# Chunks in pairs: one work item of 256 tokens in place of two of 128 in a gated linear attention with a maxout layer

**Chip, cores, metric.** One core of one Trainium2 chip. The time is device microseconds (us) of one execution, as the median of a kernel's runs. Runs marked slow are over 1.5% above the fastest run of the same kernel, or lie in a lower granted clock of TensorE; ratios use fast runs only. In what follows PE is TensorE, ACT is ScalarE, DVE is VectorE, POOL is GpSimd and SP is SyncE, which here only issues DMAs (SPq is its queue).

## The reference, cut

```python
# q, k, v, alpha: [B=4, H=8, S=768, D=48] float32
for t in range(S):
    state = alpha[:, :, t, :, None] * state + einsum('bhd,bhe->bhde', k[:, :, t], v[:, :, t])
    y[:, :, t] = einsum('bhd,bhde->bhe', q[:, :, t], state)
x = y.transpose(0, 2, 1, 3).reshape(3072, 384)
out = np.maximum(x @ w1, x @ w2) @ w_out          # w1, w2: [384, 1024], w_out: [1024, 384]
```

Both kernels use max(a, b) = b + relu(a - b): with m = w2 @ w_out, out = x @ m + relu(x @ (w1 - w2)) @ w_out. In the programs h is x @ (w1 - w2), g its relu, and op the sum that is stored. The recurrence is done in chunks of tokens: cumulative sums of log alpha by matmuls (cs), exps, q and k scaled by them (qt, kt), transposes (tp, copied to qk), masked scores (pt), a state carried from chunk to chunk (w, T), and y, which is evicted as xT.

## The kernel before, the parts that matter

An item is one chunk of 128 tokens, one token to a partition, all eight heads. There are 24 items.

```python
LD = 5                                         # loads are issued this many items ahead
def load(n):                                   # alpha, q, k, v of one chunk: rows of 192 bytes
    ...
        nc.sync.dma_start(out=t, in_=src[b, :, c*C:(c+1)*C, :].rearrange("h p d -> p h d"))

def a1(n):  nc.scalar.activation(out=logas[n % 2][:, :, 0:D], in_=loads[n][0], func=ACTF.Ln)
def p1(n):  # cs: one matmul of 384 columns, and four narrow ones (gcol)
def p4(n):  # y: v16 and T16 on 32-column tiles of the PE array, all 128 rows
...
def tstep(a, i, half):                         # op = x @ m + g @ w_out, in two halves
    ...
    if half:
        nc.scalar.copy(out=os_, in_=op)        # "outs"
        nc.sync.dma_start(out=out[t0 : t0 + C, :], in_=os_)
...
for n in range(1, NCG + 1):
    if n - 1 + LD < NCG:
        load(n - 1 + LD)                       # item n + 4, in turn n
    v1(n + 1)
    if n > 1:
        p4(n - 1); a3(n - 1)
    gap(1.05)                                  # about 1 us of h and op matmuls, from a list
    if n > 1:
        ready(n - 1)
    if n < NCG:
        a1(n + 2)                              # Ln of item n + 2
        p3(n); v3(n)
    vt(n + 1)
    gap(1.05)
    p2(n + 1); v2(n + 1)
    gap(1.05)
    p1(n + 2); a2(n + 2)
```

## Time and profile before

| | before |
|---|---|
| median of 3 runs | 163.26 us (163.16 to 163.41) |
| span of the profiled run, mean granted clock | 161.4 us, 0.989 |
| PE busy, matmuls | 139.1 us (86%), 2056 |
| one item of 128 tokens in the loop | 5.2 us, so 10.4 for two |
| load packets | 192 bytes, 15 ns each |

Three lines of the page complete them: the granted clock of PE by slices of a fortieth of the span, the chain of waits by engine, and the queue that brings instructions (packets, MB, share).

```profile
86.90 0.43 SPq L66 DMA_DIRECT2D af<-in_alpha_dram  x1
...
96.35 0.56 ACT L123 ACTIVATE loga<-af 128x384 f16<-128x384 f32 x1
```

### The profile page before, as it was taken

How to read it: one execution, taken by the hardware profiler on the slowest of the kernel's cores; microseconds unless marked ns; L12 is line 12 of the kernel's file. 1: busy time of each engine (PE TensorE's matmuls, PEld its weight loads, DVE VectorE, ACT ScalarE, POOL GpSimd, SP SyncE). 2: the span in 40 equal slices, each digit the busy share in tenths (PEclk: the TensorE clock that was granted, in tenths of full speed). 3: DMA queues.
4: the chain of work that ended last, by engine and by line, in shares of the span. 5: the costliest groups of instructions: out<-in, count | busy, mean ns of one | idle time of the engine just before them, and what ended most of it. 6: DMA issues, size and time to landing. Idle time of an engine off the chain costs nothing.

```text
span 161.4 us, 5077 instructions
## 1 busy us (share of the span) xinstructions
PE 139.1 (86%) x2056; PEld 95.2 (59%) x2056; DVE 92.9 (58%) x153; ACT 81.3 (50%) x216; POOL 91.5 (57%) x170
## 2 busy tenths in 40 slices
PE   0427169799996999999999999999999999999990
PEld 0316157467664667666766667666676667657660
DVE  4163962095668747866576766875587656841110
ACT  3302063564754574487338753775466557435341
POOL 7714555079867666777447767765376876700000
PEclk9999999999999599999999999999999999999999
DMA  5999999999989899989999979998989611012021
GB/s 106 278 411 389 275 201 162 195 188 173 199 158 235 176 201 160 225 175 231 204 224 180 222 154 236 196 230 177 216 168 220 129 55 49 0 53 97 17 84 51
DMA packets 104648, 28.65 MB, mean 178 GB/s; under 512 B 100272, under 2 KB 104368, under 8 KB 104368
## 3 DMA queue, kind: packets, MB, share of 16 engines
q1 hardware_dynamic: 104624, 28.32, 84.0%
q8 instruction: 16, 0.26, 0.7%
q14 instruction: 8, 0.07, 0.1%
HBM read 23.59 MB, written 4.72 MB: 175 GB/s over the span
## 4 chain that ended last, share of the span: by engine, by line
PE 78%; DMA 9%; ACT 3%; SPq 2%; issue 2%; DVE 2%; POOL 1%; ACTq 0%; DVEq 0%; POOLq 0%
PE h L308 22%; PE op L325 20%; DMA wof<-in_moe_w_out_dram 9%; PE op L322 8%; PE y L258 5%; PE pa L208 4%; PE y L252 3%; PE tp L192 3%; PE tp L190 3%; PE kv L217 3%; PE mp L296 2%; PE cs L130 2%; PE cs L134 2%; SPq L66 2%; DVE pt L231 1%
## 5 line engine op out<-in xcount | busy, mean ns | idle before, releaser
L157 DVE TENSOR_TENSOR qt<-qf,ep 128x384 f16<-128x384 f32 x24 | 24.4, 1016 | 34.4 <-ACT ep L146 34.4
L308 PE MATMUL h<-xT,wd 128*128 128x384 f16 (+2 forms) x264 | 40.2, 295 | 1.0 <-ACT g L313 0.6
L325 PE MATMUL op<-wo,g 128*128 128x384 f16 x192 | 38.5, 327 | 0.0
L158 POOL TENSOR_TENSOR kt<-kf,en 128x384 f16<-128x384 f32 x24 | 24.4, 1015 | 24.6 <-ACT en L145 21.1
L313 ACT ACTIVATE g<-h 128x384 f16<-128x384 f32 (+2 forms) x66 | 25.2, 410 | 10.7 <-PE h L308 10.4
L308 PEld LDWEIGHTS <-wd 128*128 128x128 f16 x264 | 22.0, 103 | 10.6 <-issue 2.6
L329 ACT COPY outs<-op 128x384 f32<-128x384 f32 x24 | 11.5, 479 | 30.9 <-PE op L325 30.9
L162 POOL CAST v<-vf 128x192 f16<-128x192 f32 x48 | 26.9, 587 | 0.0
L325 PEld LDWEIGHTS <-g 128*128 128x128 f16 x192 | 17.4, 98 | 11.1
L199 DVE COPY qk<-tp 128x1024 f16<-128x1024 f16 x24 | 16.6, 691 | 9.8 <-PE tp L192 9.0
L145 ACT ACTIVATE en<-cs 128x384 f32<-128x384 f32 x24 | 11.7, 489 | 15.7 <-PE cs L134 14.0
L176 POOL TENSOR_TENSOR T<-w,g 48x192 f16<-48x192 f32 x20 | 10.0, 501 | 14.4 <-DVE w L239 11.9
L231 DVE TENSOR_TENSOR pt<-pa,u 128x512 f16<-128x512 f32 x24 | 16.4, 685 | 2.9 <-PE pb L208 2.9
L130 PE MATMUL cs<-loga,cmat 128*128 128x384 f16 x24 | 8.1, 338 | 10.0 <-ACT loga L123 10.0
L231 DVE TENSOR_TENSOR pt<-pb,u 128x512 f16<-128x512 f32 x24 | 16.3, 678 | 0.0
L258 PE MATMUL y<-pt,v 128*32 128x128 f16 x576 | 15.7, 226 | 0.0
L322 PE MATMUL op<-m,xT 128*128 128x384 f16 x72 | 15.7, 327 | 0.0
L311 DVE TENSOR_SCALAR g<-h 128x384 f16<-128x384 f32 (+2 forms) x22 | 9.7, 440 | 10.3 <-PE h L308 10.3
L134 PEld LDWEIGHTS <-loga 128*112 128x112 f16 x96 | 9.1, 137 | 9.8 <-issue 7.8
L123 ACT ACTIVATE loga<-af 128x384 f16<-128x384 f32 x24 | 12.9, 539 | 1.8 <-DMA af<-in_alpha_dram 1.8
L265 ACT CAST xT<-y 128x384 f16<-128x384 f32 x24 | 11.8, 490 | 3.9 <-PE y L258 3.9
L258 PEld LDWEIGHTS <-v 128*32 128x32 f16 x576 | 11.8, 100 | 0.5 <-issue 0.4
(55 smaller groups left out, 185.5 us busy)
## 6 DMA issues: line engine op xcount, KB each, us to landing
af<-in_alpha_dram SPq DMA_DIRECT2D x24, 192.0 KB, 4.1
qf<-in_q_dram SPq DMA_DIRECT2D x24, 192.0 KB, 4.5
kf<-in_k_dram SPq DMA_DIRECT2D x24, 192.0 KB, 4.7
vf<-in_v_dram SPq DMA_DIRECT2D x24, 192.0 KB, 4.4
out_dram<-outs SPq DMA_DIRECT2D x24, 192.0 KB, 3.2
w2f<-in_moe_w_dram SPq DMA_DIRECT2D x1, 1536.0 KB, 8.1
w1f<-in_moe_w_dram SPq DMA_DIRECT2D x1, 1536.0 KB, 10.9
wof<-in_moe_w_out_dram SPq DMA_DIRECT2D x1, 1536.0 KB, 14.7
```

Source lines behind the costliest of these rows:

```text
L123: nc.scalar.activation(out=logas[n % 2][:, :, 0:D], in_=loads[n][0], func=ACTF.Ln)
L134: nc.tensor.matmul(cs[0:112, o : o + 2], lhsT=lp[:, r, 0:112], rhs=gcol, start=True, stop=True)
L157: nc.vector.tensor_mul(out=qts[n % 2][:, :, 0:D], in0=qf, in1=s["ep"])
L158: nc.gpsimd.tensor_mul(out=kts[n % 2][:, :, 0:D], in0=kf, in1=s["en"])
L162: nc.gpsimd.tensor_copy(out=v16[:, :, :, 32 * t : 32 * t + 16], in_=vp[:, t])
L199: nc.vector.tensor_copy(out=qk, in_=st[n]["tp"])
L231: nc.vector.tensor_mul(out=pt[:, t], in0=s["pp"][t], in1=ub)
L258: nc.tensor.matmul(y[32 * r : 32 * r + 32, i, :], lhsT=v16[:, r, i, 16 * t : 16 * t + 32], rhs=s["pt"][:, t, r, :], start=(first and t == ...
L308: nc.tensor.matmul(h[:, 0:W], lhsT=wd16[:, s, f * 128 : (f + 1) * 128], rhs=xT[:, s, a : a + W], start=(s == 0), stop=(s == 2))
L313: nc.scalar.activation(out=gts[a][:, f, 0:W], in_=h[:, 0:W], func=ACTF.Relu)
L322: nc.tensor.matmul(op, lhsT=xT[:, s, t0 : t0 + C], rhs=m16[:, s, :], start=(s == 0), stop=False)
L325: nc.tensor.matmul(op, lhsT=gts[a][:, f, i * C : (i + 1) * C], rhs=wo16[:, f, :], start=False, stop=(f == NF - 1))
```

## The change

Its intent: an item is two chunks, so that ACT, DVE and POOL run half as many instructions of twice the size, and load rows become 384 bytes by putting two neighbouring tokens on one partition. Scores, kv and y are cut into tiles of 64 rows of the PE array. The first two items are done by head halves, so that work starts before all of their data is there. The core of the diff, with cuts:

```diff
-    ldp = ctx.enter_context(tc.tile_pool(name="ldp", bufs=6))
+    ldp = ctx.enter_context(tc.tile_pool(name="ldp", bufs=4))
-    LD = 5
+    def load(n, parts=1):
+        ...                     # .rearrange("h (p j) d -> p h (j d)", j=2)
+    load(0, 2)                  # then the weights in halves, then
+    load(1, 2)
+    load(2)
+    load(3)
 ... p1: cs is eight matmuls of 192 columns (c11, c11, c11, c01 for each head half)
 ... p3: scores on 64x64 tiles, qk[64*t : 64*t+D, ...] and half the tokens (u) at a time
 ... p4: y from pt and v on 64x32 tiles, twice as many matmuls of the same streaming
+    prep_w2(0) ... p4(0); a3(0) ... fpair(0, 0..3) between the weights' casts
+    prep_wo()
+    a1(1, (0,)); p1(1, (0,)); prep_m(0); a1(1, (1,)); p1(1, (1,)); ...
+    for n in range(2, ND + 1):
+        load(n + 2)
+        v1(n + 1); v16(n + 1)
+        if n > 2: p4(n - 1); a3(n - 1)
+        tstep(n - (1 if n == 2 else 2), 1, 0)
+        a1(n + 2)
+        if n < ND: p3(n, 0); v3(n, 0)
+        tstep(n - (1 if n == 2 else 2), 1, 1)
+        if n < ND: p3(n, 1); v3(n, 1)
+        if n > 2: fpair(n - 1, 0); fpair(n - 1, 1)
+        ...                     # pkv(n), vw, vt, fpair 2 and 3, p2(n + 1), v2(n + 1)
+        if n > 2: tstep(n - 1, 0, 0)
+        p1(n + 2); a2(n + 2)
+        if n > 2: tstep(n - 1, 0, 1)
```

There are 12 items, and a turn of the loop stands for two turns of before.

## The prediction

> **What bounds the kernel now.** I read the page's busy line and slices, then a table by stage, then TensorE's timeline inside one period, then the timeline of the start.
>
> ```profile
> PE 139.1 (86%) x2056; PEld 95.2 (59%) x2056; DVE 92.9 (58%) x153; ACT 81.3 (50%) x216; POOL 91.5 (57%) x170
> ...
> PE   0427169799996999999999999999999999999990
> ...
> DMA  5999999999989899989999979998989611012021
> ```
>
> Rows of busy tenths: PE is low for 22 us, uneven to 57 us, then full. DMA is full too, up to 126 us, so a DMA bound has to be excluded. The table by stage (us; busy per engine) does it:
>
> ```profile
> 0.00:22.00 22.00, 7.31 (x82) 5.46 (x83) 11.71 (x20) 5.85 (x9) 11.75 (x25) 1.00 0.95 282
> ...
> 42.00:58.00 16.00, 14.31 (x250) 10.18 (x245) 11.33 (x21) 8.98 (x27) 11.47 (x22) 0.89 0.97 194
> ...
> 72.50:88.10 15.60, 15.60 (x249) 10.51 (x247) 10.53 (x16) 9.25 (x25) 9.16 (x17) 1.00 1.08 211
> ...
> 134.90:147.20 12.30, 12.30 (x203) 7.83 (x201) 6.23 (x10) 4.92 (x12) 4.75 (x9) 1.00 0.10 33
> ```
>
> From 57 us on, PE is covered completely while DVE, ACT and POOL are below 70%. The chain of waits runs through PE alone there. Three chunks take 15.6 us, **10.4 us for two chunks**. PE records overlap, so I took starts from the timeline:
>
> ```profile
> 73.80 0.33 PE L130 MATMUL cs<-loga,cmat 128*128 128x384 f16 x1
> 73.96 0.32 PE L134 MATMUL cs<-gcol,loga 128*112 128x2 f16 x4
> ...
> 74.84 1.15 PE L308 MATMUL h<-xT,wd 128*128 128x384 f16 x6
> 75.92 0.23 PE L208 MATMUL pa<-qk 48*128 48x128 f16 x1
> 75.93 0.23 PE L208 MATMUL pb<-qk 48*128 48x128 f16 x1
> ...
> 76.25 0.31 PE L217 MATMUL kv<-v,kt 128*64 128x48 f16 x8
> 76.49 0.66 PE L308 MATMUL h<-xT,wd 128*128 128x384 f16 x3
> ```
>
> A difference of starts is what a group costs: cs 0.16, gcol 0.25, y 0.63 (74.21 to 74.84), p3 0.43 with the gap ahead of it, kv 0.24, a 384-column matmul 0.163. Per two chunks: transposes 0.88, cs 0.33, gcol 0.5, y 1.26, p3 0.86, kv 0.40 (a sixth are skipped), h 2.62, op 22 x 0.163 = 3.58. Sum 10.43, which is the 10.4 seen: the loop holds work and no wait.
>
> The start loses most. All work of PE is 12 x 10.4 + 5 (weights) = 130 of 161.4 us; after 57 us about 4 are idle, so about 27 were lost before. The weights land last:
>
> ```profile
> 11.73 1.04 ACT L271 CAST w<-w2f 128x1024 f16<-128x1024 f32 x1 [5.60 <-DMA w2f<-in_moe_w_dram]
> ...
> 19.78 1.15 ACT L282 CAST wo<-wof 128x1152 f16<-128x1152 f32 x1 [3.85 <-DMA wof<-in_moe_w_out_dram]
> ...
> 21.41 0.48 PE L130 MATMUL cs<-loga,cmat 128*128 128x384 f16 x1 [4.62 <-ACT loga L123]
> ```
>
> [...]
> 1. [...]six h matmuls begun at 74.84 need 0.98, yet pa begins at 75.92, 0.10 later.
> 2. [...]pa and pb start 3 ns apart and a pair takes 56 ns; four 32-column tiles of y take 57 ns. No run yet has both axes at once with 32 columns.
> 3. [...]192-byte packets 15 ns, 1536-byte ones 65 ns, so by a straight line some 22 ns for 384 bytes (estimate), 280 GB/s against about 195 now.
> [...]
>
> **The change, part by part.**
>
> *Loads.* An item is 4096 packets x 22 ns / 16 = 5.7 us for two chunks, against about 8. In the loop that is off the path and worth nothing. At the start it means twice the data ahead of the weights: item 0 is moved by about 7.5 us, the weights at about 395 GB/s by 19.4 and landed by 20.6, near 1 us later than now.
>
> *PE in the loop, per item.* h, op and transposes stay. Scores: 32 matmuls of 64x64, four at once, 8 x 56 ns[...]: 0.86, as now. kv: 32, four at once, 0.45 (+0.05). y: 24 state matmuls 0.34, then 96 value matmuls on eight tiles, 12 x 57 ns = 0.68[...]: 1.25, as now. Twice the instructions for the same streaming. cs: eight matmuls of 192 columns, 8 x 0.082 = 0.66, **+0.33**, since each of two tokens of a partition needs both. gcol: eight, full 128 columns, 0.40 (-0.1). Sum **10.7 us** against 10.4: no saving on the engine that bounds.
>
> *Other engines, per item.* ACT saves in Ln, exp (four at 0.49 become two at 0.81) but takes all evictions of h (4 x 0.61); about 7.0 of 10.7. DVE: [...]copy 1.2, two masks of 1.2, w 0.7: 6.2. POOL about 7.5. All have slack, so fewer, larger instructions buy nothing by themselves.
>
> *A new wait.* PSUM units are two, of two banks. cs(n+2) needs one that v2(n+1) or the last w has just emptied. v2 is now one copy of 2048, [...]1.2 us (1024 took 0.69), starting 0.2 after the transposes. PE has one half-step of op, 0.98, between. So PE waits 1.45 - 0.98, **about 0.5 per item**; 0.76 if it is the last w. An item takes 11.2.
>
> *The start, walked by hand in program order.* Ln of the second half at 6.4 (its DMA lands), exps done 9.5, kt and v casts on POOL 12.3, kv and scores 13.5, masks 16.6, T16 16.8, y 18.3, xT 19.4. Then ACT is in series: w2 second half 1.5 (20.9), first two g (22.1); wd second half waits for the w2T copies on DVE (23.6), g 25.6, wo 27.05; only then Ln of item 1. PE: m 28.2, second half's p1 at 30.7, since ACT puts m's copy ahead of its Ln; scores of item 1 36.8, y 43.3, h until 49.2, p1(3) 50.7, loop entered at 53.5. Its first turn has no h work to hide masks behind, 5.1 of work in 8.2: 61.7. At that time the kernel before has y of 7 chunks and h of 6; the walk has 4 and 4, with ops level. So the start gains nothing, though two chunks are done before 20 us instead of one.
>
> *The end.* Turns 3 to 9 at 11.2 = 78.4; turn 10 without cs 9.6, turn 11 without transposes 8.8, turn 12 9.3 + 0.5 exposed, last copy and store 3.4 (as now from 157.55). 61.7 + 110.0 = 171.7 span, and 1.9 between span and time: **173.6**.
>
> **Rivals.**
> *A, the start really gains.* If ACT's serial piece from 19.4 to 27 overlaps better than my walk, PE starts in earnest near 22 with two chunks behind it: 22 + 122 of PE work + 4 = 148 span, 150 to 156 in time with some waits. For it: PE idles about 15 of the first 22 us, and the change fills it with h of item 0. Against: Ln of item 1 stands behind wo and four g on ACT in program order.
> *B, no wait in the loop and tighter y.* Without the 0.5, and y 1.0[...], the loop is 10.45 per item and the time 165 with my start. [...]Against: the eviction chain above is plain in program order.
> *C, issue bound.* If 96 + 96 small instructions of y and 32 of kv don't run eight at once but at about 14 ns each, 0.7 more per item: 180. Against: starts 2 to 3 ns apart within a group now.
> *D, DMA was the bound.* Then 384-byte rows give up to 30%. Against: no wait for a load inside the loop, PE covered.
>
> **Range and chances.** The walk gives 173.6. I take 4 us or so off: its start counts each wait in full, and the order of the code looks tuned, which speaks for A. Predicted 169.0. Low end 157 holds most of A, high end 176 leaves C out. Faster than 160.0 needs A in large part: 0.22. Within 2% (to 166.5) is B or half of A: 0.22. Slower: 0.56.
>
> **What would show it.** Right: windows of a full item in the loop of 10.9 to 11.5 us; a PE gap near 0.5 before cs, ended by DVE's qk copy or w; cs 0.66 per item; xT of item 0 near 19, Ln of item 1 after wo near 27; p4 of item 2 near 62; load packets near 22 ns. Wrong: a loop of 10.4 or less without the gap (B); PE full from 25 us (A); y over 1.8 us per item (C); waits of PE's suppliers for loads in the loop (D).

## More of the kernel before

```profile
PEclk9999999999999599999999999999999999999999
...
q8 instruction: 16, 0.26, 0.7%
...
PE 78%; DMA 9%; ACT 3%; SPq 2%; issue 2%; DVE 2%; POOL 1%; ACTq 0%; DVEq 0%; POOLq 0%
```

The chain is PE. Almost all of its DMA share is the weights at the start. The waits list Ln (L123) as waiting for alpha once (us in total, times, longest):

```profile
ACT loga L123 <- DMA af<-in_alpha_dram: 1.8, 1, 1.8
```

## The result, and the profile after

| | before | after |
|---|---|---|
| median | 163.26 us | 186.13 us (185.62 to 188.78, 4 runs) |
| ratio of fast runs | | 1.1375, 95% interval 1.1324 to 1.1426 |
| span, mean clock of the profiled run | 161.4, 0.989 | 184.8, 0.981 (fast) |
| PE busy | 139.1 (86%) | 146.7 (79%) |
| two chunks in the loop | 10.4 | 12.2 (median turn) |

A ratio here is the mean time of one kernel's fast runs over that of the other's in the same rounds, so it isn't quite the ratio of the medians quoted. One run of the changed kernel (188.78, clock 0.954) was slow and is left out of it. The record has a fifth run, of 184.98 us and fast; the four fast ones have a median of 185.65, which is used below. The kernel is slower, which the prediction held for likeliest, but some 10 us beyond the end of its range and some 12 beyond the sum of its walk (173.6).

The page of the changed kernel, the lines that answer to those of before:

```profile
PE 146.7 (79%) x3091; PEld 105.0 (57%) x3091; DVE 84.6 (46%) x95; ACT 84.8 (46%) x160; POOL 88.2 (48%) x139
...
PE   0256754757796788998997988979989789999992
...
PEclk9999995799999999999999999999999999999999
...
q8 instruction: 24, 0.39, 0.9%
...
PE 44%; DMA 19%; ACT 15%; DVE 11%; issue 6%; SPq 2%; ACTq 0%
```

Four things are to be seen. PE has its row of nines only in the last slices. Its clock is halved in the seventh and eighth slice (27.6 to 34.5 us in the records); the 9s before 24.2 us say nothing, as the clock records of this profile begin there, and twelve matmuls of h at 21.3 us take nearly twice what they take later (below). There are half as many instruction packets again (24 for 16), and PE runs half as many instructions again (6182 matmuls and weight loads for 4112). And the chain is no longer PE's: DMA has 19% of it, all of it alpha loads. The waits say whose (us in total, times, longest):

```profile
ACT loga L157 <- DMA af<-in_alpha_dram: 32.8, 9, 4.3
...
PE h L413 <- ACT outs L433: 6.2, 6, 1.2
```

The chain in order of time (start, us, what) shows one turn of this:

```profile
92.44 0.36 SPq L434
...
92.84 4.90 DMA af<-in_alpha_dram
...
97.77 0.04 ACT loga L157
97.81 0.71 issue
98.52 0.47 ACT outs L433
...
99.03 0.81 PE h L413 x6
```

SP issues a store, then alpha of the item that is to be worked on next. Alpha lands 4.9 us later, and Ln starts. Behind it ACT copies op out, and only then does PE run its next six matmuls of h. The timelines of ACT and PE show the same from the side of those who wait (start, us, engine, line, operation, and in brackets the idle time before it and what ended it):

```profile
92.62 1.05 ACT L364 CAST xT<-y 128x384 f16<-128x384 f32 x2 [0.21 <-PE y L339]
97.77 0.84 ACT L157 ACTIVATE loga<-af 128x768 f16<-128x768 f32 x1 [4.09 <-DMA af<-in_alpha_dram]
98.52 0.46 ACT L433 COPY outs<-op 128x384 f32<-128x384 f32 x1
...
93.93 0.99 PE L429 MATMUL op<-wo,g 128*128 128x384 f16 x5
...
96.97 0.83 PE L413 MATMUL h<-xT,wd 128*128 128x256 f16 x6
99.03 0.81 PE L413 MATMUL h<-xT,wd 128*128 128x256 f16 x6 [1.23 <-ACT outs L433]
```

PE ended op at about 94.9, but its copy runs at 98.52: in program order it stands behind Ln, for which ACT sits idle from 93.67 to 97.77 (4.09 us). The relus of h stand behind Ln too, the four PSUM banks of op and h stay taken, and PE stops for 1.23 us.

The cause in the code is one line. Before, turn n loads item n + 4 and takes Ln of n + 2, two turns apart. After, turn n loads item n + 2 and takes Ln of the same item n + 2 a few lines below.

The table by stage for one turn (window; total, then busy time and count of PE, PEld, DVE, ACT and POOL; clock; DMA share; GB/s) gives PE 11.0 of 12.2 us:

```profile
92.50:104.70 12.20, 10.97 (x255) 7.97 (x247) 6.06 (x6) 6.18 (x12) 5.02 (x7) 1.00 0.69 164
```

The rest is in the start: xT of item 1 comes at 51.2 and xT of item 2 at 68.4. The walk had y of these items from 43.3 and 61.7 on; with 1.4 us from y to xT (an estimate; the trace has 1.5) that is 44.7 and 63.1. Two timelines, of ACT and of PE:

```profile
30.61 0.52 ACT L157 ACTIVATE loga<-af 128x384 f16<-128x384 f32 x1
...
35.04 0.53 ACT L157 ACTIVATE loga<-af 128x384 f16<-128x384 f32 x1
...
21.32 2.72 PE L413 MATMUL h<-xT,wd 128*128 128x256 f16 x12 [1.17 <-ACT xT L364]
...
31.93 2.69 PE L396 MATMUL mp<-wo,w2T 128*128 128x384 f16 x8
```

Ln of item 1 runs at 30.6 and 35.0 (walked: 27.05 and, with p1 of the second half at 30.7, some 30.1). Between the two stand eight matmuls of m that take 2.69 us; at the full clock eight take 1.46, as at 36.05 in the same trace, or 1.3 from start to start (in the kernel before, 24 of them take 4.06). The twelve matmuls of h at 21.32 are as slow: the same twelve take 1.48 in the loop. So PE seems to be at half speed there too (2.72 us against 1.48), though no record says so.

### The profile page after: what moved, and what is told of

It reads as the page before. It is cut to its first block, busy times and chain, and to the rows that moved or that the text cites. A ratio compares the mean times of both kernels' runs of the same rounds, so it can differ in the third digit from the quotient of the medians.

```text
span 184.8 us, 6870 instructions
## 1 busy us (share of the span) xinstructions
PE 146.7 (79%) x3091; PEld 105.0 (57%) x3091; DVE 84.6 (46%) x95; ACT 84.8 (46%) x160; POOL 88.2 (48%) x139
## 4 chain that ended last, share of the span: by engine, by line
PE 44%; DMA 19%; ACT 15%; DVE 11%; issue 6%; SPq 2%; ACTq 0%
DMA af<-in_alpha_dram 19%; PE h L413 12%; PE op L429 8%; PE tp L235 5%; DVE qk L248 4%; PE y L339 4%; ACT en L198 3%; ACT outs L433 3%; PE op L426 3%; ACT ep L198 3%; DVE qt L210 3%; DVE pt L273 3%; ACT loga L157 2%; PE cs L173 2%; PE mp L396 2%
## 5 line engine op out<-in xcount | busy, mean ns | idle before, releaser
L413 PE MATMUL h<-xT,wd 128*128 128x256 f16 x288 | 38.1, 281 | 9.5 <-ACT outs L433 6.2
L210 DVE TENSOR_TENSOR qt<-qf,ep 128x768 f16<-128x768 f32 (+1 forms) x14 | 24.9, 1793 | 36.8 <-ACT ep L198 36.8
L213 POOL TENSOR_TENSOR kt<-kf,en 128x768 f16<-128x768 f32 (+1 forms) x14 | 22.7, 1629 | 33.6 <-ACT en L198 31.2
L413 PEld LDWEIGHTS <-wd 128*128 128x128 f16 x288 | 27.1, 100 | 15.9 <-issue 8.5
L273 DVE TENSOR_TENSOR pt<-pp,cmask 128x1024 f16<-128x1024 f32 x24 | 29.0, 1219 | 7.0 <-PE pp L261 6.7
L415 ACT ACTIVATE g<-h 128x512 f16<-128x512 f32 x48 | 26.6, 602 | 9.5 <-PE h L413 8.8
L248 DVE COPY qk<-tp 128x2048 f16<-128x2048 f16 (+1 forms) x14 | 15.0, 1070 | 27.0 <-PE tp L235 27.0
L157 ACT ACTIVATE loga<-af 128x768 f16<-128x768 f32 (+1 forms) x14 | 10.5, 751 | 34.4 <-DMA af<-in_alpha_dram 32.8
L329 POOL TENSOR_TENSOR T<-w,g 48x192 f16<-48x192 f32 x40 | 20.1, 502 | 12.0 <-DVE w L308 10.6
L222 POOL CAST v<-vf 128x384 f16<-128x384 f32 x24 | 23.1, 987 | 0.1
L339 PE MATMUL y<-pt,v 64*32 64x128 f16 x1152 | 12.5, 229 | 0.0
L339 PEld LDWEIGHTS <-v 64*32 64x32 f16 x1152 | 10.7, 92 | 1.4 <-issue 0.2
```

The lines of the kernel that those rows point to most:

```text
L210: nc.vector.tensor_mul(out=qts[n % 2][:, :, r, 0:D], in0=qf[:, r].rearrange("p h (j d) -> p j h d", j=2), in1=s["ep"][:, :, r])
L213: nc.gpsimd.tensor_mul(out=kts[n % 2][:, :, r, 0:D], in0=kf[:, r].rearrange("p h (j d) -> p j h d", j=2), in1=s["en"][:, :, r])
L222: nc.gpsimd.tensor_copy(out=v16s[n % NB][:, :, :, :, 32 * t : 32 * t + 16], in_=vp[:, t])
L248: nc.vector.tensor_copy(out=s["qk"].rearrange("p h w j r c -> p h (w j r c)")[:, hh], in_=s["tp"].bitcast(FP16)[:, hh])
L273: nc.vector.tensor_mul(out=s["pt"][:, h], in0=s["pp"].rearrange("p t (r x) -> p (t r) x", r=2), in1=cmask.rearrange("p j x -> p (j x)").un ...
L329: nc.gpsimd.tensor_mul(out=T16[ps, u2, :, :, 16 * t : 16 * t + 16], in0=ws[ps], in1=gs[ps])
```

## The experiments

Each was correct against the reference. The median of the kernel before in the same rounds is in square brackets.

### 1. The load one turn earlier

```diff
+    load(4)                      # just before tstep(0, 0, 0)
-        load(n + 2)
+        load(n + 3)
```

> The changed kernel with each item's load issued one turn earlier (item n+3 in turn n instead of n+2, item 4 ahead of the first store). Theory L (loads come late: the load of alpha is issued in the same turn in which Ln needs it, behind two stores on the same queue, so Ln waits some 4 us in ACT's queue with the copies of op and the relus of h behind it, and PE stands for want of free h banks): Ln's waits for alpha in the loop (30 us in all) go to under 3, the 1.4 us PE gap ahead of the fourth h pair goes, the 0.5 wait of cs for the qk copy comes back; a turn falls from 12.3 to about 11.3 us; 7 x 1.0 and some 3 to 4 at turn 2 and 3: time 174 to 176. Rival P (the two PSUM units and ACT's evictions set the pace, the wait for loads only sits in slack): a turn stays at 12 or more, time 183 or more.

Measured: 178.67 us (177.75 to 179.78) [163.22], ratio 1.0948, interval 1.0886 to 1.1009. A turn fell to 11.1 us in the mean, and of the waits of Ln one is left, in the start:

```profile
ACT loga L157 <- DMA af<-in_alpha_dram: 3.1, 1, 3.1
```

In the loop, Ln now runs right behind xT, and the copy of op waits for nothing that a load holds up:

```profile
92.04 1.04 ACT L364 CAST xT<-y 128x384 f16<-128x384 f32 x2 [0.21 <-PE y L339]
92.93 0.85 ACT L157 ACTIVATE loga<-af 128x768 f16<-128x768 f32 x1
94.42 0.48 ACT L433 COPY outs<-op 128x384 f32<-128x384 f32 x1 [0.63 <-ACT loga L157]
```

The table by stage shows PE covered for the whole of this turn, the shortest; two of three turns are 11.2 to 11.3, with a wait of 0.34 us for the qk copy:

```profile
91.90:102.80 10.90, 10.90 (x258) 8.04 (x248) 6.15 (x6) 6.57 (x12) 5.11 (x7) 1.00 0.76 184
```

So the late load costs **7.0 us** (185.65 less 178.67, fast runs alone), and the start, unchanged, keeps the rest. The time is 2.7 above what was expected.

### 2. Ln later in the turn, the load where it was

```diff
-        a1(n + 2)                # after tstep(., 1, 0)
...
+        a1(n + 2)                # just before p1(n + 2)
         p1(n + 2)
```

> The changed kernel with loads untouched and Ln of item n+2 moved in program order to just ahead of its matmul cs, behind the relus of the turn. Theory L in the form that the order in ACT's queue does the damage: the load still comes as late, but nothing stands behind Ln, so the PE gap goes and a turn falls to 11.2 to 11.5, time 175 to 178. If the load's lateness itself is the limit: cs then waits for Ln and the turn stays near 12.3, time 184 to 187.

Measured: 179.17 us (178.30 to 180.69) [163.22], ratio 1.0985 (1.0915 to 1.1056). Ln waits little, and a turn is 11.1 us in the mean:

```profile
ACT loga L157 <- DMA af<-in_alpha_dram: 5.3, 2, 3.1
```

The loads are as late as in the changed kernel here (an alpha is issued at 93.12, there at 92.84). What hurt was not the transfer, nor the bandwidth, but that Ln held up the work behind it.

### 3. The kernel before with its loads later

```diff
-    LD = 5
+    LD = 3
```

> The kernel before with its load distance cut from LD = 5 to LD = 3, so that the load of chunk n+2 is issued in the turn in which Ln(n+2) runs, as the change does. Theory L: Ln waits for alpha 2 to 4 us in many turns of 5.2, time 180 or more (if all of it shows, 24 x 2 = up to 210). Rival P: PE stays the bound and the kernel runs at 163 to 167.

Measured: 174.13 us (173.87 to 175.24) [163.22], ratio 1.0686 (1.0626 to 1.0747). With the load of item n + 2 in the turn of its Ln, the kernel before gets the same wait in the same place:

```profile
ACT loga L123 <- DMA af<-in_alpha_dram: 28.6, 13, 2.8
```

The mechanism holds, and its size is smaller than expected (180 or more).

### 4. Stores issued by ACT, so that SP isn't held up by them

```diff
-            nc.sync.dma_start(out=out[t0 : t0 + C, :], in_=os_)
+            nc.scalar.dma_start(out=out[t0 : t0 + C, :], in_=os_)
```

> The changed kernel with its stores issued from ACT's queue instead of the queue of the loads; load distance untouched in the program. Theory L with the store as what holds the load: loads then wait only for a free buffer and run 2 items ahead, Ln's waits go as in the run with earlier loads, time 173 to 177, plus some 0.4 us of ACT issue per store which has slack. If instead the distance in program order (buffers) is what makes the load late: as the changed kernel, 184 to 187.

Measured: 179.31 us (178.92 to 180.67) [163.22], ratio 1.0999 (1.0939 to 1.1059). Alphas in the loop are issued at 37.2, 43.2 and 57.1 instead of 61.1, 66.6 and 80.8, and Ln waits 3.2 us in all. So `load(n + 2)` is as late as it is because a store before it in SP's queue waits for a copy of op. Three cures in three places land within 0.7 us of each other. The expected gain was larger by 2 us at least; with the start as late as measured, I read this as the loop being cured and the rest left as it was.

### 5. A start in another order, with the load of 1

```diff
+    prep_w2(1)                   # before p4(0)
-    fpair(0, 2); fpair(0, 3); prep_wo()     # all ahead of Ln of item 1
+    ... a1(1, (0,)); p1(1, (0,)); fpair(0, 2); a1(1, (1,)); p1(1, (1,)); fpair(0, 3) ...
+    ... prep_wo(); then prep_m between the transposes of item 1; a1(2), a1(3), v1(2) earlier
```

> The run with earlier loads (178.7 us), and its start reordered: both halves of the cast of w2 ahead of xT of item 0 on ACT, Ln and cs of item 1 ahead of the cast of wo and of the three products m, Ln of item 2 before the op steps. Theory S (the start is a queue of ACT and PE work in program order, as the prediction walked it, and the data of item 1 lie ready from 23 to 26 us): Ln of item 1 moves from 30.8 and 35.3 to some 24 and 27, y of item 1 from 50 to near 43, the throttled stretch of 28 to 35 us shrinks or goes; total 170 to 174. Rival H (the start is bound by the chain of latencies through DVE and POOL, not by the order): y of item 1 stays within 2 us of 50 and the time is 176 to 179.

Measured: 174.65 us (173.90 to 174.91) [163.99], ratio 1.0647 (1.0578 to 1.0716), so 4.0 us below experiment 1. Ln of item 1 runs at 26.5 and 29.8. No slice of this profile shows a halved clock, but its clock records begin at 38.7 us, and from 23.2 us up to there PE is at half speed: twelve matmuls of h at 23.2 take 2.77 us (1.48 in the loop), eight of m at 36.3 take 2.66 (1.46 at 39.2). So the gain is the order's, not the clock's. xT of item 1 comes at 48.4 instead of 51.4; 43 had been expected for y of it, and it was about 47.

### 6. Experiment 5, and two repairs of the loop

```diff
-        tstep(n - (1 if n == 2 else 2), 1, 0)      # and the same of (1, 1)
+        if n != 3:
+            tstep(n - (1 if n == 2 else 2), 1, 0)
...
-        p1(n + 2); a2(n + 2)
         if n > 2: tstep(n - 1, 0, 1)
+        p1(n + 2); a2(n + 2)
```

The first repair answers a fault that I had read past: at n = 2 the step is that of item 1, and at n = 3, with n - 2, it is that of item 1 again. The changed kernel does this piece twice (25 stores instead of 24). The second puts op work between the qk copy and cs.

> As the run with the reordered start, and in the loop the second half-step of op ahead of cs, and the op step of item 1 that the program does twice (in turn 2 and again in turn 3) done once. Theory: the gap of 0.34 us ahead of cs in every second turn goes, a turn falls from 11.1 to 10.9 (1.5 us over the loop), and turn 3 loses 1.8 us of PE work: 2.5 to 3.5 us below the run with the reordered start alone. Rival: cs later makes the exps and qt later, DVE then holds the masks and the turn stays at 11.1: gain 1.8 or less.

Measured: 173.58 us (171.27 to 175.33) [163.99], ratio 1.0499 (1.0384 to 1.0614). Two of the four runs are slow (174.20 and 175.33); the fast ones are 172.95 and 171.27, some 2.5 us below experiment 5, the low end of what was expected, but the two intervals overlap. Its profiled run was slow (clock 0.951, halved from 23.9 to 41.0 us), so its start tells nothing; from 41.0 on the clock is full. A turn of its loop is 10.7 to 11.0 us, 10.8 in the mean against 11.1 in experiment 1. That fits the wait for the qk copy which the prediction had put at 0.5 per item: in experiment 1 it is 0.34 in two turns of three, 0.23 per turn, and here it is gone.

### 7. The changed kernel without head halves

```diff
-    load(0, 2) ... load(1, 2)
+    load(0) ... load(1)
-    for h in range(2):
-        a1(0, (h,)); p1(0, (h,)) ...                # the same for item 1
+    a1(0); p1(0); a2(0); v1(0) ...
```

> The changed kernel with the first two items loaded and computed whole instead of by head halves, nothing else. If the halves do what they are meant to: xT of item 0 moves from 20.2 to 21.5 to 22.5 (exps and products of 768 columns instead of two of 384 staggered), item 1 likewise, total 187 to 190. Rival: the first items hang on the weights and on ACT's order, and halves only add instructions: 184 to 187.

Measured: 186.86 us (185.50 to 188.37) [163.99], ratio 1.1371 (1.1276 to 1.1466): the same as with them (one run, 188.37, is slow and not in the ratio). xT of item 0 comes at 20.2 in both. The halves buy nothing that can be measured.

### 8. PE kept busy in the start, with the load of 1

```diff
+    warm(16)      # dummy matmuls of 256 columns into a PSUM bank, where PE idled in the start
...
+    warm(18)
```

> The run with earlier loads, plus 34 matmuls of 256 columns without use in two gaps of PE at the start (16 ahead of the second half of h of item 0, 18 ahead of the first cs of item 1), results unused. Theory W (the throttled stretch of 28 to 35 us is what the walk of the start missed, the clock being halved there[...]): the record of the clock shows no halved stretch, the first product m takes 1.3 instead of 2.7 us, y of item 1 comes 2 to 3 us earlier, total 175.5 to 177. Rival: the work there is latency of other engines, the clock costs under 1 us: 178 to 179.5.

Measured: 182.40 us (180.41 to 183.39) [163.99], ratio 1.1147 (1.1059 to 1.1235). One run (183.39) is slow. The start does what was expected: the clock isn't halved, the matmuls of m take 1.46 instead of 2.72 us, and xT of item 1 comes at 48.4, 3.0 earlier than in experiment 1. That the clock is halved where PE has idled was the author's estimate and isn't shown (in the changed kernel PE stands from 24.9 to 26.8 us and from 28.7 to 31.2, and the clock is halved from 27.6 to 34.5), and not all of this is shown to be the dummy matmuls' work. Here PE is at full speed from 19.8 us on, before the first of them, and so it is in experiment 10, which has the same start without them: there one stretch of 3.4 us is halved (30.2 to 33.6), and xT of item 1 comes at 49.4. Against that profile the gain is 1.0; the other 2.0 vary from run to run. The total is a miss. At 66.8 PE stops in the middle of a group, for 3 us and with no wait:

```profile
66.38 0.41 PE L261 MATMUL pp<-qk 48*64 48x128 f16 x15
69.80 0.24 PE L261 MATMUL pp<-qk 48*64 48x128 f16 x1 [3.01 <-issue]
```

Behind it the clock is halved once more (71.0 to 74.4), and item 3 is where it was in experiment 1 (81.4 against 80.7). That explains why the gain is lost in the profiled run, with a span of 178.6 against 178.0 in experiment 1. But this run (180.41) is the fastest of the four here, and that of experiment 1 (179.78) the slowest there. In the median of the fast runs experiment 8 is 3.4 us slower (182.10 against 178.67), and no profile shows where; this stays open.

### Holes of PE without a wait

Such holes stand in the profiles of most of these kernels. I counted PE's instructions, from 0, up to each: in experiments 1, 2 and 5 to 10, wherever a hole is over 0.5 us (1.72 in 5, 1.42 in 6, 3.01 in 8, 1.66 in 9), the first instruction after it is number 449 or 1729, both 193 past a multiple of 256. Three shorter ones (0.27 to 0.42 us, in experiments 4, 6 and 9) lie at other numbers that are 193 past a multiple. Each of these holes ends 1.2 to 1.7 us after the end of a 16 KB packet of the instruction queue. There are about 256 PE instructions to such a packet: 4112 and 16 packets in the kernel before, 6182 and 24 in the changed one, and experiment 12 has 2304 more than experiment 1, and 33 packets in place of 24. That PE runs out of instructions there, where it has just passed many short ones, is my reading; the profile names nothing that it waits for. Experiments 12 and 13 test this.

### 9. The best combination

Experiment 6 with `prep_wd(1)` earlier, and exps and products of item 1 ahead of the last two pairs of h of item 0.

```diff
+    prep_wd(1)                   # before p4(0)'s h work
+    a2(1, ...); v1(1, ...)
     fpair(0, 2)
     fpair(0, 3)
     prep_wo()
```

> As the run with all changes (173.6 us median, 171.3 its fastest), with exps and products of item 1 ahead of the last two h pairs of item 0 in the start, where that run let them stand behind those relus until 33 us. Theory S: qt of item 1 from 34 to about 29, y of item 1 from 48 to 50 down to 45 or 46, total 168 to 171; still over the kernel before, since a turn costs 10.8 for 10.4 and the start is not full. Rival H (latency of DVE and POOL, not order): y of item 1 within 1 us, time 171 to 174.

Measured: 172.28 us (169.77 to 172.59) [163.26]. Two of the four runs are marked slow (172.41 and 172.59), so no ratio is given; the fast ones are 172.15 and 169.77. xT of item 1 comes at 45.7, of item 2 at 61.1. The first turn takes 13.3 us, with a hole of 1.66 and a clock halved from 66.8 to 70.2, the later full ones 10.6 to 11.3. It has the lowest median that I found, though its fast runs overlap those of experiment 6, and it doesn't reach the kernel before.

### 10. The double step alone, with the load of 1

```diff
+        if n != 3:
             tstep(n - (1 if n == 2 else 2), 1, 0)    # and (1, 1)
```

> The run with earlier loads (178.7), with the op step of item 1 done once instead of twice. If turn 3 is bound by PE: 1.8 us less, 176.5 to 177.3. If turn 3 is a chain of latencies that this step only fills: less than 0.7 us gained.

Measured: 177.97 us (177.29 to 179.18) [163.26], ratio 1.0867 (1.0752 to 1.0983), 0.7 below experiment 1 in the median, with intervals that overlap. The turn concerned takes 11.7 us from xT to xT instead of 12.3. So the double work seems worth about half a microsecond; a hole in this turn (69.6 to 71.06) is 0.4 longer than in experiment 1 and may take part of it.

### 11. The kernel before, one step later only

```diff
-    LD = 5
+    LD = 4
```

> The kernel before with LD = 4: each load one turn (5.2 us) ahead of its Ln instead of two. A load lands 4.1 to 4.7 us after issue, so by theory L this is just enough: 163 to 166, with a few us of waits for alpha in all; clearly below the 174.1 of LD = 3. If it is 168 or more, the loads' own queue is long enough that a lead of one turn doesn't hold.

Measured: 163.04 us (162.36 to 163.60) [163.26], ratio 0.9947 (0.9852 to 1.0041): the same. LD of 5, 4 and 3 gives 163.3, 163.0 and 174.1. It is not a matter of more or less: a turn's distance is enough, and none is 11 us.

### 12 and 13. Instruction supply: 128 small matmuls a turn, or ten large ones

Both stand on experiment 1 and put a filler ahead of cs in turns 3 to 11.

```diff
+    # 12: 32 x 4 matmuls of 64 columns, four at once on 32-column tiles (256 PE instructions)
+    # 13: 10 matmuls of 256 columns (20 PE instructions)
```

> The run with earlier loads (178.7), plus in each turn from 3 to 11 128 matmuls without use of 64 columns on four 32-column tiles, ahead of cs: near 1 us of PE streaming, 256 more PE instructions (a weight load and a matmul each). In earlier traces PE stood without any wait at always the same place in the program, 193 past a multiple of 256 PE instructions, until 5.7 to 6.1 us after it passed the same mark 256 instructions sooner. Theory F (PE can't take its program faster than 256 instructions in some 5.2 to 5.8 us): a turn has about 760 PE instructions, three blocks, and takes 15.5 or more: 7 x 4.4 = 31 and up, time 203 to 215. Rival (the holes are something else): only the streaming time counts, 9 x 1.1, less the 0.34 gaps it fills: 186 to 189.

> The control: the same place in each turn filled with 10 matmuls of 256 columns, 1.09 us of PE streaming and 20 instructions. Under both theories 186 to 189; theory F has this run at least 15 us below the run with 128 small ones, the rival has both within 3 us.

Measured: small 195.14 us (193.78 to 195.94), ratio 1.1882 (1.1761 to 1.2002); large 185.47 (184.41 to 186.59), ratio 1.1310 (1.1206 to 1.1413) [163.65]. A turn is 12.98 and 11.87 us in the mean of six. In the loop of 12, PE stops seven times within those six turns, by 0.3 to 0.8 us each, at numbers that are multiples of 256 apart, and in 13 only once, in turn 3, which is before the six. One of them, in the timeline of PE of experiment 12:

```profile
106.13 0.47 PE L339 MATMUL y<-pt,v 64*32 64x128 f16 x33
107.08 0.73 PE L339 MATMUL y<-pt,v 64*32 64x128 f16 x63 [0.48 <-issue]
```

The break falls inside 96 matmuls that all wait for the same things. The stops came with the small filler, as theory F has it, and their size was misjudged: the two were to differ by 15 us or more and differ by 9.7. Nor is all of that shown to be supply. The six turns are 77.9 us in 12 and 71.2 in 13, a difference of 6.7, and PE stands still for 4.2 of it; the rest lies inside groups of short matmuls that take longer (y at 157.94 has no hole and takes 1.23 us from start to start, against 0.93 in 13). With the small filler a turn is 506 + 256 = 762 PE instructions in 12.98 us, or 4.4 us per 256. The loop of experiment 1 takes 11.1 for 506, or 5.6 per 256, so it is above that as a whole; that only bursts of short matmuls outrun the supply is an estimate from these two figures.

## Why the prediction was right or wrong

The direction was right, the size wrong by more than the range. The span of 184.8 against the walk's 171.7 leaves 13.1 us: 6.8 for late loads (the spans of the changed kernel and of experiment 1, 184.8 and 178.0), 5.3 for the start (xT of item 2 at 68.4 against 63.1), and 1.0 for the rest.

- **"*Loads.* ... In the loop that is off the path and worth nothing."** This step failed, and it is the largest part. The text looked at how long a transfer takes and not at when it is issued. The new diff has `load(n + 2)` and `a1(n + 2)` in one turn; I carried the distance of the kernel before over to it. Experiments 1, 2 and 4 each cure it by another way, and 3 and 11 bring it into the kernel before and keep it out. The sizes were near: packets of 384 bytes took 25 ns in the median (22 in the first 10 us, as the straight line gave), against 15 for 192 bytes and 65 to 67 for 1536. Where loads alone ran (about 31 to 38 us) they moved 261 GB/s, not the 280 estimated. The weights' 395 GB/s fits the kernel before, which moved 406 from 8 to 12 us and 387 from 12 to 15.9.
- **Rival D, "Against: no wait for a load inside the loop".** For the changed kernel that was false, by the same mistake: Ln waits 32.8 us for loads, the sign that the prediction had named for D. But D itself, a bound of DMA, is not what happened: with the data just as late, experiment 2 has the short turn.
- **"Sum 10.7 us against 10.4: no saving on the engine that bounds."** Right. With loads in time, turns are 10.8 to 11.3, and 10.7 to 11.0 where the wait for the qk copy is filled (6). Within the sum, y takes 1.38 (91.12 to 92.50) against 1.25, and cs with gcol 0.87 (89.35 to 90.22) against 1.06. Rival C (y at 14 ns a matmul) is out: 96 take 0.93 us. Scores (0.86) and y (1.25) hold an allowance for pauses, the author's estimate from the 0.10 us ahead of pa at 75.92; experiment 1 has as much ahead of its scores at 94.27, where five matmuls of op from 93.35 need 0.82.
- **"About 0.5 per item", the wait for the eviction.** Right in kind, found as 0.34 in two turns of three (1), though the copy took 1.22 us, and was given 1.2; so a turn is 11.1 and not 11.2.
- **"Fewer, larger instructions buy nothing by themselves."** Right: DVE, ACT and POOL were below half of the span in the changed kernel and the time rose.
- **The start, "loop entered at 53.5 ... 61.7".** Too early by 5.3. About 3 us are matmuls at half speed: the walk gave those of h and m their durations at the full clock, 1.3 for eight of m, and the trace has 2.69. In experiment 8, where none of the start is slow from 19.8 us on, xT of items 1 and 2 comes 3.0 earlier; 2.3 of the 5.3 are left, and no run takes them apart. "The start gains nothing" was right, and rival A wrong: xT of chunks 4 and 5 comes at 68.4, and before at 49.8 and 53.7. Taking "4 us or so off" the sum in favour of A went in the wrong direction.
- **"All have slack", the durations at twice the width.** These were estimates. The changed kernel has 0.81 us for an exp of 768 columns (0.81 given), 0.60 for a relu of 512 (0.61) and 1.22 for a mask (1.2). qt of 768 took 2.03, and DVE was busy for 6.06 in the turn of 12.20 shown above (6.2 given). In the kernel before, qt of 384 took 0.56 us three times (at 6.10, 35.51 and 49.91) and 1.07 to 1.13 the other 21; POOL was at work those three times too, and what makes it longer elsewhere isn't shown. The forecast hardly rests on it.
- **Not in the working.** The step done twice (10: 0.7 us of median) and the holes of PE without a wait (4.2 us in six turns of 12). "Twice the instructions for the same streaming" was noted and taken to be free.

Why the form is slower even when repaired (9): an item of its loop costs 10.6 to 11.3 against 10.4, and its start is behind (xT of item 2 at 61.1, against 53.7 for the same tokens before). What the change saves lies on engines that had slack. How much of the start could still be won by other orders stays open, and so do the unexplained microseconds of experiment 8.

## What to carry to other kernels

When a loop is rewritten with larger items, write down for each load in which turn it is issued and in which its first reader stands, and do so for the new code, not from the old profile; a "no wait for loads" there says nothing about a loop with another distance. Ln, placed early in ACT's program, turned a late load (4.09 us of waiting in the turn shown) into a wait of everything behind it, so either the load goes a turn earlier or the reader later; both cured this alike (178.67 and 179.17 us). And find out on which engine the saved instructions lie: here savings beside the engine that bounds didn't count. A walk of a start must allow for matmuls at half speed, and for their varying from run to run (2.7 us or 1.46 for the same eight of m); and a row of 9s for the clock is to be checked against the durations of the matmuls under it.
